# A shorter ending by column tiles of TensorE, ten unused matmuls in its waits, and two instruction programs aligned, in a decode attention kernel

## The chip, the cores and the metric

The kernel runs on one core of a Trainium2 chip. The metric is device time in microseconds, the median of several runs. The profile is one execution taken by the hardware profiler; its times count from the first instruction of that execution.

## The reference, cut to what matters

One decode step: two sequences of one token, a cached attention block with 32 heads of 8192 positions, and a small ReLU block beside it, both from the same normalised input.

```python
xn = _layernorm(x)                                    # x: [2, 1, 512]
# A: wq [512, 4096], K and V caches [2, 32, 8192, 128], wo [4096, 512]
q = (xn @ wq) per head                                # [2, 32, 1, 128]
p = softmax(q k^T * 128**-0.5);  o = p v
# B: w1 [512, 1792], w2 [1792, 512]
return x + o @ wo + relu(xn @ w1) @ w2
```

All inputs are bf16. K and V are 268 MB of the 280.5 MB that are read; wq, wo, w1 and w2 are the rest.

## The kernel before, in words

**The loop.** Sixteen turns work on four heads each. A turn brings 8 MB of K into the one buffer `ks` and 8 MB of V into the one buffer `vs`. TensorE transposes K (L278), VectorE and ScalarE copy the transposes out of PSUM (L446), TensorE makes the scores (L285), VectorE finds the maxima, ScalarE makes the exponentials with their sums in `RS`, and TensorE multiplies by V (L352). GpSimd hands out the queries of the next turn. All orders are written out by hand, with semaphores; there is no scheduler.

**The queue.** All large transfers are issued by SyncE on one queue, in program order: K, V, K, V and so on, and, as soon as the last K has been transposed, w1 (L191), w2 (L192) and wo (L195) into the space that K leaves in `ks`. wo comes in pieces along its 32 row groups `j`, cut at 0, 18, 26, 30 and 32, with one semaphore a piece, so that its product can begin before all of it is there. The matmuls of a piece wait for that piece (`piece[c]`).

**The ending**, after the last product with V, on TensorE in program order: the denominators (L373, four float32 matmuls against `onesh`); the input itself put into the accumulator `fin` (L379); the first product of the ReLU block (L390, 56 matmuls whose weights are w1 columns taken 14 elements apart, two columns of `xz` moving); the transposes of the attention output (L402); its move into the row layout of wo (L406); the second ReLU product (L417 from `hT`, 56 matmuls); the output projection (L417 from `OX`, 128 matmuls); a last transpose (L437). In L417 the weight matrix is TensorE's stationary operand, 128 columns at a time, and the two sequences are the two moving columns. VectorE works between these steps: the normalised output `OTn` (L511 to L529), the ReLU `hT` (L533), the copies `Ob` (L537), `OX` (L539), `yT` (L543) and `osb` (L545). SyncE then writes the output (L197).

**Unused matmuls.** `unused` (L308) multiplies the identity into a PSUM bank that nobody reads. The loop already has some in its waits.

Of the kernel before, what the change touches and what calls it, by code (L numbers as in the profile page):

```python
# [7 lines left out]
ALU = mybir.AluOpType  # L8
ACTF = mybir.ActivationFunctionType
AX = mybir.AxisListType  # L10

U = 4
# [4 lines left out]
TR = (21, 25)  # L17
BC = 32
FILL = 5
PZ = 4  # L20
ON_ACT = (0, 3, 5)


# [1 line left out]
def kernel(  # L25
# [35 lines left out]
    QG = H * Dh // 512  # L61
    QH = 512 // Dh
    Z = (QG - 1) * Bsz

    inv_sqrt = float(Dh) ** -0.5
    eps = 1e-5
# [3 lines left out]
    def sb(shape, dt, name):  # L70
        return ctx.enter_context(nc.sbuf_tensor(name, shape, dt))
# [4 lines left out]
    def sem(name):  # L76
        return tc.alloc_semaphore(name)
# [10 lines left out]
    kT = [sb([P, EG, P], bf16, f"kT{i}") for i in range(NG)]  # L88
    identb = sb([P, P], bf16, "identb")
    sel = sb([H, DQ, P], bf16, "sel")  # L90
    onesh = sb([P, U, P], f32, "onesh")
    onesb = sb([1, P], bf16, "onesb")
    eps_t = sb([P, 1], f32, "eps_t")
    xsb = sb([Bsz, D], bf16, "xsb")
# [3 lines left out]
    rinv = sb([Bsz, 1], f32, "rinv")  # L98
    xn = sb([Bsz, KT, P], bf16, "xn")

    xz = sb([P, KT, 2 * Z + Bsz], bf16, "xz")
    qs = sb([QG * Bsz, 512], bf16, "qs")
    qb = sb([P, N], bf16, "qb")
    q4 = sb([P, U], bf16, "q4")
# [2 lines left out]
    mcol = sb([P, 2], bf16, "mcol")  # L107
    mx = sb([1, 2, U], bf16, "mx")
    nm = sb([P, 2, U], f32, "nm")
    RS = sb([P, 2, NP], f32, "RS")  # L110
    NM = sb([P, 2, N], f32, "NM")
    OTf = sb([P, 2, N], f32, "OTf")
    lo = sb([P, N], f32, "lo")
# [6 lines left out]
    OG = sb([P, 2, N], f32, "OG")  # L120
    OTn = sb([P, Bsz, H], bf16, "OTn")
    Ob = sb([H, Bsz, Dh], bf16, "Ob")
    OX = sb([P, WJ, Bsz], bf16, "OX")
    hT = sb([P, FJ, Bsz], bf16, "hT")
    yT = sb([P, Bsz, KT], bf16, "yT")
    osb = sb([Bsz * KT, P], bf16, "osb")

# [23 lines left out]
    K_all = A_k_cache.rearrange("b h (m kk) d -> (b h m) (kk d)", kk=KB)  # L151
    V_all = A_v_cache.rearrange("b h (m kk) d -> (b h m) (kk d)", kk=KB)
    wo_v = A_wo.rearrange("(p j) n -> p j n", j=WJ)
    cuts = (0, 18, 26, 30, WJ)
    NC = len(cuts) - 1

    KSPLIT = (0, 2, NP - 1)
    VSPLIT = (1, 2)
    NL = 16 * NP
    piece = [(dX, 32), (dQ, 32)] + [(sem(f"dWo{c}"), 16) for c in range(2, NC)]  # L160
    qp = ot[0:QG * Bsz, :]
    tpq = ms[:, 0:N // 2].bitcast(bf16).rearrange("p (l c) -> p l c", l=QH)
    tpx = tp[0][:].rearrange("p g k -> p (g k)")[:, 0:KT * Bsz].rearrange(
        "p (kt b) -> p kt b", b=Bsz
    )
    hp = ms[:, 128:128 + FJ * Bsz].rearrange("p (j b) -> p j b", b=Bsz)
    ox = ms[:, 256:256 + Bsz * WJ]
    fin = Sc[:, 512:512 + KT * Bsz]

# [41 lines left out]

    @(lambda f: f(nc.gpsimd))
    def _(g):
        g.memset(identb[:], 0.0).then_inc(sG, 1)
        g.memset(sel[:], 0.0).then_inc(sG, 1)
        g.memset(onesh[:], 0.0).then_inc(sG, 1)
        g.wait_ge(sG, 1)
        g.affine_select(
            out=identb[:], in_=identb[:], compare_op=ALU.not_equal, fill=1.0,
            base=0, pattern=[[-1, P]], channel_multiplier=1,  # L220
        ).then_inc(sI, 1)
        g.wait_ge(sG, 2)
        g.affine_select(
            out=sel[:], in_=sel[:], compare_op=ALU.not_equal, fill=1.0,
            base=0, pattern=[[-1, DQ], [1, P]], channel_multiplier=-DQ,
        ).then_inc(sI, 1)
        g.wait_ge(sI, 2)
        for k in range(PZ - 1):
            g.memset(prm[:, k * KB // PZ:(k + 1) * KB // PZ, :], 0.0)
        g.memset(prm[:, KB - KB // PZ:KB, :], 0.0).then_inc(sG, 1)  # L230
        g.wait_ge(sG, 4)
        for u in range(U):
            g.memset(onesh[u * HP:(u + 1) * HP, u, :], 1.0).then_inc(sI, 1)
            g.wait_ge(sI, 3 + u)
        g.wait_ge(sV, 100)
        for t in range(NP):
            if t > 0:
                g.wait_ge(sS, 2 * t)
            g.tensor_copy(q4[:], qb[:, U * t:U * t + U]).then_inc(sQ1, 1)
            for d, split in ((dK, KSPLIT), (dV, VSPLIT)):  # L240
                if t not in split:
                    g.wait_ge(d[0], 16 * (t + 1)).then_inc(d[1], 16)
        g.wait_ge(dO, 16).then_inc(sG, 1)


    @(lambda f: f(nc.tensor))
    def _(pe):
# [119 lines left out]
                            warm(4)  # L367
            advance(pe, regs)

        pe.wait_ge(sI, 2 + U)  # L370
        dbp = Sc[:, 0:2 * N].rearrange("p (t u) -> p t u", u=U)
        for u in range(U):
            t = pe.matmul(  # L373
                dbp[:, :, u], lhsT=onesh[:, u, :], rhs=RS[:].rearrange("p i t -> p (i t)"),
                start=True, stop=True,
            )
        t.then_inc(sH, 1)
        for k in range(KT):
            pe.matmul(  # L379
                fin[:, k * Bsz:(k + 1) * Bsz],  # L380
                lhsT=xsb[:, k * P:(k + 1) * P],
                rhs=identb[0:Bsz, 0:Bsz],
                start=(k == 0),
                stop=False,
            )
        pe.wait_ge(dW1, 16)
        w1_v = w1_sb.rearrange("p kt (f j) -> p kt j f", j=FJ)
        for j in range(FJ):
            for kt in range(KT):
                i = pe.matmul(  # L390
                    hp[:, j, :],
                    lhsT=w1_v[:, kt, j, :],
                    rhs=xz[:, kt, Z:Z + Bsz],
                    start=(kt == 0),
                    stop=(kt == KT - 1),
                )
        i.then_inc(sF, 1)

        pe.wait_ge(sV, 108)
        tO = tp[0][0:H, 0:Bsz, :]  # L400
        for b in range(Bsz):
# [10 lines left out]
            )  # L412
        t.then_inc(sH, 1)

        def project(w, j, x, last=False):
            for k in range(KT):
                t = pe.matmul(  # L417
                    fin[:, k * Bsz:(k + 1) * Bsz],
                    lhsT=w[:, j, k * P:(k + 1) * P],
                    rhs=x[:, j, :],  # L420
                    start=False,
                    stop=(last and k == KT - 1),
                )
            return t

        pe.wait_ge(sF, 2)
        pe.wait_ge(dW2, 16)
        for j in range(FJ):
            project(w2_sb, j, hT)
        pe.wait_ge(sV, 110)  # L430
        for c in range(NC):
            pe.wait_ge(*piece[c])
            for j in range(cuts[c], cuts[c + 1]):
                t = project(wo_sb, j, OX, j == WJ - 1)
        t.then_inc(sH, 1)
        pe.wait_ge(sV, 111)
        pe.transpose(  # L437
            tp[1][0:Bsz * KT, 0, :], yT[:].rearrange("p b c -> p (b c)"), identb[:]
        ).then_inc(sH, 1)

    def kcopies(eng, act, h):
# [6 lines left out]

    @(lambda f: f(nc.vector))
    def _(v):  # L450
        v.memset(eps_t[:], eps).then_inc(sV, 1)
        v.memset(onesb[:], 1.0)
        v.memset(xz[:], 0.0).then_inc(sZ, 1)
        v.wait_ge(dX, 16)
        v.bn_stats(out=stats[:], in_=xsb[:]).then_inc(sV, 1)
        v.wait_ge(sV, 2)
# [50 lines left out]
        def both(ap):  # L507
# [21 lines left out]
        v.tensor_tensor(  # L529
            out=OTn[:].rearrange("p b h -> p (b h)"), in0=OG[:, 0, :], in1=OG[:, 1, :], op=ALU.add  # L530
        ).then_inc(sV, 1)
        v.wait_ge(sF, 1)
        v.tensor_scalar(  # L533
            out=hT[:], in0=hp, scalar1=0.0, scalar2=None, op0=ALU.max,
        ).then_inc(sF, 1)
        v.wait_ge(sH, 2)
        v.tensor_copy(Ob[:], tp[0][0:H, 0:Bsz, :]).then_inc(sV, 1)  # L537
        v.wait_ge(sH, 3)
        v.tensor_copy(  # L539
            OX[:], ox.rearrange("p (b j) -> p j b", b=Bsz)  # L540
        ).then_inc(sV, 1)
        v.wait_ge(sH, 4)
        v.tensor_copy(yT[:], fin.rearrange("p (c b) -> p b c", c=KT)).then_inc(sV, 1)  # L543
        v.wait_ge(sH, 5)
        v.tensor_copy(osb[:], tp[1][0:Bsz * KT, 0, :]).then_inc(sE, 1)  # L545


    @(lambda f: f(nc.scalar))
    def _(a):
        a.wait_ge(sV, 3)  # L550
        a.activation(
            out=rstd[:], in_=mv[:, 1:2], func=ACTF.Sqrt, bias=eps_t[:Bsz], scale=1.0
        ).then_inc(sA, 1)

        a.copy(nm[:, 0, 0:1], eps_t[:]).then_inc(sO, 1)
        regs = counters(a, mybir.EngineType.Activation)
        reg, g, h = regs[0], regs[1:3], regs[3:]
        with a.Fori(0, NP) as t:
            kcopies(a, True, h)
            for i in range(2):  # L560
                a.wait_ge(sB, g[i])
                a.copy(nm[:, i, :], bc[:, i, :]).then_inc(sN, 1)  # L562
                a.wait_ge(sN, g[i])
                for u in range(U):
                    own = slice(u * HP, (u + 1) * HP)
                    k = slice(i * KB // 2, (i + 1) * KB // 2)
                    x = a.activation(  # L567
                        out=prm[own, k, u],
                        in_=S[own, k, u],
                        func=ACTF.Exp,  # L570
                        bias=nm[own, i, u:u + 1],
                        scale=1.0,
                        accum_out=RS[own, i, bass.ds(t, 1)],
                    )
# [6 lines left out]
        a.activation(out=F[:], in_=df[:], func=ACTF.Exp, scale=1.0).then_inc(sA, 1)  # L581
# [1 line left out]
_INS = ['A_x', 'A_k_cache', 'A_v_cache', 'A_wq', 'A_wo', 'B_x', 'B_w1', 'B_w2']  # L583
_OUTS = [((2, 1, 512), 'bfloat16')]
# [25 lines left out]
```

## Time and profile before

| | us |
|---|---|
| median of 4 runs (658.56 to 658.89) | 658.58 |
| the profiled execution | 658.49 |
| its span, first to last instruction | 656.7 |
| last K transposed, w1 issued | 624.2 |
| last product with V ends on TensorE | 642.5 |
| last piece of wo landed | 653.04 |
| last matmul of the projection over | 653.48 |
| output write issued | 654.27 |

The profiled execution is 1.8 us longer than its span; that much lies around the first and last instruction. In the tables of the profile a row is a group of instructions: start, time, engine, line, operation, output and inputs, shapes, count, and in brackets the idle time of the engine before it. PE is TensorE's matmuls, PEld its weight loads, DVE is VectorE, ACT ScalarE, POOL GpSimd, SP SyncE. The time of one matmul in these rows runs from its start to the end of its passage; matmuls overlap, so what counts for a stream of them is the distance of their starts.

### The profile page before, as it was taken

The numbers are of one execution on the slowest core, as the hardware profiler recorded it, in microseconds if no ns is written. First come the engines' busy times: TensorE is split into PE (matmuls) and PEld (weight loads), VectorE is DVE, ScalarE is ACT, GpSimd is POOL, SyncE is SP. The second block draws the span as 40 slices with busy tenths as digits, with TensorE's granted clock in tenths as the row PEclk, the third lists the DMA queues.
The fourth block names the chain that finished last, engine by engine and source line by source line (L and its number), as shares of the span: only waits on it lengthen the run. The fifth ranks groups of instructions, "written<-read, shape, count | busy, mean of one in ns | idle before, by whom it ended". The sixth has DMA issues, their size and how long they took to land.

```text
span 656.7 us, 27972 instructions
## 1 busy us (share of the span) xinstructions
PE 611.4 (93%) x13071; PEld 540.0 (82%) x13071; DVE 261.8 (40%) x503; ACT 290.8 (44%) x532; POOL 7.2 (1%) x33
## 2 busy tenths in 40 slices
PE   2876999999999999999999999999999999999997
PEld 0575899968979798897969879796997979799987
DVE  1440353507235071633507154260715417072721
ACT  1332445526344363543527354353725435372730
POOL 2000000000000000000000000000000000000000
PEclk9998899999999999999999999999999999999997
DMA  9999999999999999999999999999999999999996
GB/s 381 450 437 413 418 431 431 461 415 431 431 435 427 443 427 439 427 435 443 423 435 435 435 443 423 427 431 447 427 439 423 435 443 423 431 431 424 459 393 288
DMA packets 6367, 280.66 MB, mean 427 GB/s; under 512 B 722, under 2 KB 724, under 8 KB 980
## 3 DMA queue, kind: packets, MB, share of 16 engines
q1 hardware_dynamic: 6352, 280.50, 99.0%
q8 instruction: 8, 0.13, 0.1%
q14 instruction: 3, 0.02, 0.0%
q10 hardware_dynamic: 4, 0.00, 0.0%
HBM read 280.50 MB, written 0.00 MB: 427 GB/s over the span
## 4 chain that ended last, share of the span: by engine, by line
DMA 54%; PE 43%; issue 2%; ACT 1%; SPq 0%; DVE 0%; ACTq 0%
DMA ks<-in_A_k_cache_dram 50%; PE tp L278 34%; DMA ks<-in_A_wo_dram 4%; PE ot L352 4%; PE Sc L285 4%; PE ms L308 1%; ACT L446 0%; DVE mcol L493 0%; ACT kT L446 0%; PE tp L308 0%; SPq L195 0%; PE ms L297 0%; PE ms L303 0%; SPq L192 0%; SPq L183 0%
## 5 line engine op out<-in xcount | busy, mean ns | idle before, releaser
L446 DVE COPY kT<-tp 128x1024 bf16<-128x1024 bf16 x320 | 209.1, 687 | 246.2 <-PE tp L278 240.5
L278 PEld LDWEIGHTS tp<-identb,ks 128*128 128x128 bf16 x4096 | 228.8, 98 | 22.4 <-DMA ks<-in_A_k_cache_dram 19.2
L278 PE MATMUL tp<-identb,ks 128*128 128x128 bf16 x4096 | 232.0, 219 | 15.5 <-DMA ks<-in_A_k_cache_dram 13.1
L446 ACT COPY kT<-tp 128x1024 bf16<-128x1024 bf16 x192 | 188.1, 1014 | 127.9 <-PE tp L278 127.8
L285 PE MATMUL Sc<-q,kT 128*128 128x64 bf16 (+8 forms) x4096 | 133.2, 191 | 4.5 <-issue 4.5
L352 PE MATMUL ot<-prm,vs 128*128 128x64 bf16 x4096 | 130.9, 193 | 3.8 <-issue 3.3
L285 PEld LDWEIGHTS Sc<-q,kT 128*128 128x128 bf16 x4096 | 128.6, 98 | 6.0 <-issue 4.8
L352 PEld LDWEIGHTS ot<-prm,vs 128*128 128x128 bf16 x4096 | 126.8, 97 | 5.8 <-issue 3.6
L308 PE MATMUL ms<-identb 128*128 128x512 bf16 x340 | 75.6, 379 | 0.0
L493 DVE TENSOR_REDUCE mcol<-Sc 32x1 bf16<-32x128 f32 x128 | 37.1, 290 | 93.9 <-PE Sc L285 92.6
L567 ACT ACTIVATE prm<-Sc,nm 32x128 bf16<-32x128 f32 x128 | 68.9, 539 | 5.4
L562 ACT COPY nm<-ms 128x4 f32<-128x4 f32 x32 | 5.2, 163 | 140.3 <-PE ms L303 140.3
L308 PEld LDWEIGHTS ms<-identb 128*128 128x128 bf16 x340 | 32.4, 98 | 37.1 <-issue 0.2
L578 ACT COPY OTf<-ot 128x8 f32 x16 | 2.6, 165 | 72.7 <-PE ot L352 72.7
L567 ACT ACTIVATION_READ_ACCUMULATOR prm<-Sc,nm x128 | 32.1, 251 | 0.0
L446 ACT ACT_TABLE_LOAD x16 | 20.5, 1283 | 3.7 <-issue 3.6
L308 PE MATMUL tp<-identb 128*128 128x512 bf16 x80 | 20.8, 391 | 0.0
L257 PE MATMUL ot<-vs,xz 128*16 128x512 bf16 x32 | 9.8, 482 | 8.6 <-DMA vs<-in_A_wq_dram 8.6
L257 PEld LDWEIGHTS ot<-vs,xz 128*16 128x16 bf16 x32 | 3.4, 107 | 14.6 <-issue 12.6
L500 DVE TENSOR_REDUCE mx<-ms 1x4 bf16<-1x128 bf16 x32 | 8.9, 279 | 14.3 <-PE ms L297 14.3
L297 PEld LDWEIGHTS ms<-identb,mcol 128*1 128x1 bf16 x32 | 2.5, 79 | 12.8 <-ACT prm L567 11.2
L308 PEld LDWEIGHTS tp<-identb 128*128 128x128 bf16 x80 | 6.7, 98 | 6.2 <-issue 0.8
(64 smaller groups left out, 57.3 us busy)
## 6 DMA issues: line engine op xcount, KB each, us to landing
ks<-in_A_k_cache_dram SPq DMA_DIRECT2D x6, 4096.0 KB, 22.3
vs<-in_A_v_cache_dram SPq DMA_DIRECT2D x4, 4096.0 KB, 21.6
vs<-in_A_wq_dram SPq DMA_DIRECT2D x1, 4096.0 KB, 12.3
ks<-in_B_w_dram SPq DMA_DIRECT2D x2, 1792.0 KB, 16.4
ks<-in_A_wo_dram SPq DMA_DIRECT2D x1, 2304.0 KB
ks<-in_A_wo_dram SPq DMA_DIRECT2D x1, 1024.0 KB, 25.6
ks<-in_A_wo_dram SPq DMA_DIRECT2D x1, 512.0 KB, 26.4
ks<-in_A_wo_dram SPq DMA_DIRECT2D x1, 256.0 KB, 26.6
```

Of the source, the lines that this page charges most:

```text
L257: i = pe.matmul(qp, lhsT=xz[:, kt, Z - g * Bsz:Z - g * Bsz + QG * Bsz], rhs=vs[:, (kt * QG + g) * 512:(kt * QG + g + 1) * 512], start=(g = ...
L278: t = pe.transpose(tp[e % 4][:, i, :], ks[:, kk * Dh:(kk + 1) * Dh], identb[:])
L285: t = pe.matmul(Sc[:, U * kk:U * (kk + n)], lhsT=kT[e][:, i, :], rhs=rep(q4[:], n), start=True, stop=True,)
L297: pe.transpose(trp[:, i * P:(i + 1) * P], mcol[:, i:i + 1], identb[:]).then_inc(sT, 1)
L308: pe.matmul(out, lhsT=identb[:], rhs=identb[:].rearrange("p (o k) -> p o k", o=1).to_broadcast([P, 4, P]), start=True, stop=True,)
L352: t = pe.matmul(oh[:, i, :], lhsT=vs[:, kk * Dh:(kk + 1) * Dh], rhs=rep(prm[:, kk, :], REP), start=(first == 0), stop=(first == KB // 2 - 1),)
L446: fn(kT[e][:], tp[e % 4][:]).then_inc(kR[e % HG], 1)
L493: m = v.tensor_reduce(out=mcol[own, i:i + 1], in_=S[own, i * KB // 2:(i + 1) * KB // 2, u], axis=AX.X, op=ALU.max,)
L500: v.tensor_reduce(out=mx[:, i, :], in_=trp[:, i * P:(i + 1) * P].rearrange("o (u m) -> o u m", u=U), axis=AX.X, op=ALU.max, negate=True,). ...
L562: a.copy(nm[:, i, :], bc[:, i, :]).then_inc(sN, 1)
L567: x = a.activation(out=prm[own, k, u], in_=S[own, k, u], func=ACTF.Exp, bias=nm[own, i, u:u + 1], scale=1.0, accum_out=RS[own, i, bass.ds( ...
L578: a.copy(OTf[:, :, bass.ds(t * U, U)], oh[:, :, 0:U]).then_inc(sO, 1)
```

## The change

The ending is rewritten; the loop stays as it is. Three products change sides: the few columns of the activations become the stationary operand, filled up to 32 columns with zeros, and the weight matrix moves past, 448 or 512 columns in one matmul. Each such matmul uses a quarter of TensorE's columns and writes 32 partitions of PSUM, and consecutive matmuls go round the four quarters. This holds for w1 (16 matmuls), w2 (14) and the first 22 of 32 row groups of wo. The four partial sums in `y` are copied by VectorE to `ys` and added by four float32 matmuls against the selection `sel2`. The last ten row groups of wo are done in the old way. wo is cut at 0, 14, 22, 26, 30 and 32, five pieces. Seven unused matmuls follow the first piece and three the second. w1's product is copied by ScalarE (`hb`), transposed by 14 small matmuls, and the ReLU is done in four instructions, one for each quarter. The denominators need one float32 matmul, because `RS` now has a column for each head. GpSimd sets `RS`, `ones`, `hT` and `OX` to constants. The programs of VectorE and GpSimd begin with an instruction to the loader to place them at a multiple of 128 instructions, with a branch over what lies between.

```diff
+FETCH = 128
+PAUSE = (7, 3)
-    cuts = (0, 18, 26, 30, WJ)
+    cuts = (0, 14, 22, 26, 30, WJ)
+    WIDE = 2
@@ GpSimd
+        g.addr_align(FETCH, max_nops=0)
...
+        g.memset(RS[:], 0.0).then_inc(sG, 1)
+        g.memset(ones[:], 1.0).then_inc(sG, 1)
+        g.memset(hT[:], 0.0).then_inc(sG, 1)
...
+        g.wait_ge(sS, 2 * NP)
+        g.memset(OX, 0.0).then_inc(sI, 1)
@@ TensorE
-        for u in range(U):
-            t = pe.matmul(dbp[:, :, u], lhsT=onesh[:, u, :], rhs=RS[:]...)
+        pe.matmul(Sc[:, 0:2 * N], lhsT=ones[:], rhs=RS[:]...).then_inc(sH, 1)
         pe.wait_ge(dW1, 16)
-        for j in range(FJ):
-            for kt in range(KT):
-                i = pe.matmul(hp[:, j, :], lhsT=w1_v[:, kt, j, :], rhs=xz[:, kt, Z:Z + Bsz], ...)
+        for kt in range(KT):
+            for c in range(TC):
+                i = pe.matmul(tile(hp, c)[:, 0:FJ * CT], lhsT=xz[:, kt, Z:Z + CT],
+                    rhs=w1_sb[:, kt, c * FJ * CT:(c + 1) * FJ * CT], ...)
+        pe.matmul(tile(y, 0), lhsT=identb[0:Bsz, 0:CT], rhs=xsb[:], start=True, stop=False)
+        pe.wait_ge(sF, 2)
+        for j in range(FJ):
+            t = pe.matmul(hq[...], lhsT=hb[:, j, :], rhs=rows, start=True, stop=True)
...
-        for j in range(FJ):
-            project(w2_sb, j, hT)
+        for j in range(FJ):
+            pe.matmul(tile(y, j % TC), lhsT=hT[:, j, :], rhs=w2_sb[:, j, :], ...)
         pe.wait_ge(sV, 110)
-        for c in range(NC):
-            pe.wait_ge(*piece[c])
-            for j in range(cuts[c], cuts[c + 1]):
-                t = project(wo_sb, j, OX, j == WJ - 1)
+        for i in range(WIDE):
+            pe.wait_ge(*piece[i])
+            for j in range(cuts[i], cuts[i + 1]):
+                t = pe.matmul(tile(y, j % TC), lhsT=OX[:, j, :], rhs=wo_sb[:, j, :], ...)
+            if i == WIDE - 1:
+                t.then_inc(sH, 1)
+            for k in range(PAUSE[i]):
+                unused(ms[:])
+        for i in range(WIDE, NC):
+            if i == WIDE:
+                pe.wait_ge(sF, 5)
+                for k in range(KT):
+                    pe.matmul(fin[:, k * Bsz:(k + 1) * Bsz],
+                        lhsT=ys[:, k * P:(k + 1) * P], rhs=sel2[:], ...)
+            pe.wait_ge(*piece[i])
+            for j in range(cuts[i], cuts[i + 1]):
+                for k in range(KT):
+                    t = pe.matmul(fin[...], lhsT=wo_sb[:, j, k * P:(k + 1) * P],
+                        rhs=OX[:, j, 0:Bsz], ...)
@@ VectorE
+        v.addr_align(FETCH, max_nops=0)
+        v.wait_ge(sI, 1)
+        v.tensor_reduce(out=sel2[:], in_=identb[:]..., op=ALU.add)
...
-        v.tensor_scalar(out=hT[:], in0=hp, scalar1=0.0, op0=ALU.max).then_inc(sF, 1)
+        for c in range(TC):
+            m = v.tensor_scalar(out=hT[c * CT:(c + 1) * CT, :, 0:Bsz],
+                in0=hq...[:, :, c, :], scalar1=0.0, op0=ALU.max)
+        m.then_inc(sF, 1)
...
+        v.tensor_copy(ys, y).then_inc(sF, 1)
@@ ScalarE, after the loop
+        a.wait_ge(sF, 1)
+        a.copy(hb, hp[:, 0:FJ * CT].rearrange("p (f j) -> p j f", j=FJ)).then_inc(sF, 1)
```

More of the change, by code (lines that the diff above doesn't have):

```diff
@@ L19 @@
 FILL = 5
-PZ = 4
+CT = 32
+FETCH = 128
+PAUSE = (7, 3)
 ON_ACT = (0, 3, 5)
@@ L63 @@
     Z = (QG - 1) * Bsz
+    TC = P // CT
+    assert D == 512 and FJ * CT <= 512 and FJ * TC * Bsz <= 512
     inv_sqrt = float(Dh) ** -0.5
@@ L90 @@
     sel = sb([H, DQ, P], bf16, "sel")
-    onesh = sb([P, U, P], f32, "onesh")
+    ones = sb([P, P], f32, "ones")
     onesb = sb([1, P], bf16, "onesb")
@@ L99 @@
     xn = sb([Bsz, KT, P], bf16, "xn")
-    xz = sb([P, KT, 2 * Z + Bsz], bf16, "xz")
+    xz = sb([P, KT, max(2 * Z + Bsz, Z + CT)], bf16, "xz")
     qs = sb([QG * Bsz, 512], bf16, "qs")
@@ L109 @@
     nm = sb([P, 2, U], f32, "nm")
-    RS = sb([P, 2, NP], f32, "RS")
+    RS = sb([P, 2, NP, U], f32, "RS")
     NM = sb([P, 2, N], f32, "NM")
@@ L122 @@
     Ob = sb([H, Bsz, Dh], bf16, "Ob")
-    OX = sb([P, WJ, Bsz], bf16, "OX")
-    hT = sb([P, FJ, Bsz], bf16, "hT")
+    hT = sb([P, FJ, CT], bf16, "hT")
+    sel2 = sb([P, Bsz], f32, "sel2")
     yT = sb([P, Bsz, KT], bf16, "yT")
@@ L159 @@
     NL = 16 * NP
-    piece = [(dX, 32), (dQ, 32)] + [(sem(f"dWo{c}"), 16) for c in range(2, NC)]
+    piece = [(dX, 32), (dQ, 32), (dK[0], NL + 16), (dK[1], NL + 16)] + [
+        (sem(f"dWo{c}"), 16) for c in range(4, NC)
+    ]
     qp = ot[0:QG * Bsz, :]
@@ L165 @@
     )
-    hp = ms[:, 128:128 + FJ * Bsz].rearrange("p (j b) -> p j b", b=Bsz)
+    hp = tp[2][:].rearrange("p g k -> p (g k)").bitcast(f32)
+    y = tp[1][:].rearrange("p g k -> p (g k)").bitcast(f32)
+    hb = kT[0][:].rearrange("p g k -> p (g k)")[:, 0:FJ * CT].rearrange(
+        "p (j f) -> p j f", j=FJ
+    )
+    hq = tp[3][:].rearrange("p g k -> p (g k)").bitcast(f32)[0:CT, 0:FJ * TC * Bsz]
+    OX = kT[2][:].rearrange("p g k -> p (g k)").rearrange("p (j c) -> p j c", c=CT)
+    ys = kT[1][:].rearrange("p g k -> p (g k)").bitcast(f32)
     ox = ms[:, 256:256 + Bsz * WJ]
@@ L213, in _ @@
     def _(g):
+        g.addr_align(FETCH, max_nops=0)
         g.memset(identb[:], 0.0).then_inc(sG, 1)
         g.memset(sel[:], 0.0).then_inc(sG, 1)
-        g.memset(onesh[:], 0.0).then_inc(sG, 1)
         g.wait_ge(sG, 1)
@@ L227, in _ @@
         g.wait_ge(sI, 2)
[L228 to L231, printed above, removed]
-        for u in range(U):
-            g.memset(onesh[u * HP:(u + 1) * HP, u, :], 1.0).then_inc(sI, 1)
-            g.wait_ge(sI, 3 + u)
+        g.memset(prm[:], 0.0).then_inc(sG, 1)
+        g.memset(RS[:], 0.0).then_inc(sG, 1)
+        g.memset(ones[:], 1.0).then_inc(sG, 1)
+        g.memset(hT[:], 0.0).then_inc(sG, 1)
+        g.wait_ge(sG, 6)
         g.wait_ge(sV, 100)
@@ L368, in _, with tile @@
             advance(pe, regs)
[L370 to L385, printed above, removed]
+        pe.matmul(
+            Sc[:, 0:2 * N], lhsT=ones[:], rhs=RS[:].rearrange("p i t u -> p (i t u)"),
+            start=True, stop=True,
+        ).then_inc(sH, 1)
+        def tile(ap, c):
+            return ap[c * CT:(c + 1) * CT, :]
         pe.wait_ge(dW1, 16)
-        w1_v = w1_sb.rearrange("p kt (f j) -> p kt j f", j=FJ)
-        for j in range(FJ):
-            for kt in range(KT):
+        for kt in range(KT):
+            for c in range(TC):
                 i = pe.matmul(
-                    hp[:, j, :],
-                    lhsT=w1_v[:, kt, j, :],
-                    rhs=xz[:, kt, Z:Z + Bsz],
+                    tile(hp, c)[:, 0:FJ * CT],
+                    lhsT=xz[:, kt, Z:Z + CT],
+                    rhs=w1_sb[:, kt, c * FJ * CT:(c + 1) * FJ * CT],
                     start=(kt == 0),
@@ L397, in _ @@
         i.then_inc(sF, 1)
+        pe.matmul(
+            tile(y, 0), lhsT=identb[0:Bsz, 0:CT], rhs=xsb[:], start=True, stop=False
+        )
+        pe.wait_ge(sF, 2)
+        rows = identb[:].rearrange("p (c r) -> p c r", c=TC)[:, :, 0:Bsz]
+        for j in range(FJ):
+            t = pe.matmul(
+                hq[:, j * TC * Bsz:(j + 1) * TC * Bsz].rearrange("p (c b) -> p c b", c=TC),
+                lhsT=hb[:, j, :], rhs=rows, start=True, stop=True,
+            )
+        t.then_inc(sF, 1)
         pe.wait_ge(sV, 108)
@@ L413, in _ @@
         t.then_inc(sH, 1)
[L415 to L426, printed above, removed]
+        pe.wait_ge(sF, 4)
         pe.wait_ge(dW2, 16)
         for j in range(FJ):
-            project(w2_sb, j, hT)
-        pe.wait_ge(sV, 110)
-        for c in range(NC):
-            pe.wait_ge(*piece[c])
-            for j in range(cuts[c], cuts[c + 1]):
-                t = project(wo_sb, j, OX, j == WJ - 1)
+            c = j % TC
+            pe.matmul(
+                tile(y, c), lhsT=hT[:, j, :], rhs=w2_sb[:, j, :],
+                start=(0 < j < TC), stop=False,
+            )
+        pe.wait_ge(sV, 110)
+        for i in range(WIDE):
+            pe.wait_ge(*piece[i])
+            for j in range(cuts[i], cuts[i + 1]):
+                t = pe.matmul(
+                    tile(y, j % TC), lhsT=OX[:, j, :], rhs=wo_sb[:, j, :],
+                    start=False, stop=(j >= cuts[WIDE] - TC),
+                )
+            if i == WIDE - 1:
[6 more added lines that the diff above has]
+                for k in range(KT):
+                    pe.matmul(
+                        fin[:, k * Bsz:(k + 1) * Bsz],
+                        lhsT=ys[:, k * P:(k + 1) * P],
+                        rhs=sel2[:],
+                        start=(k == 0),
+                        stop=False,
+                    )
+            pe.wait_ge(*piece[i])
+            for j in range(cuts[i], cuts[i + 1]):
+                for k in range(KT):
+                    t = pe.matmul(
+                        fin[:, k * Bsz:(k + 1) * Bsz],
+                        lhsT=wo_sb[:, j, k * P:(k + 1) * P],
+                        rhs=OX[:, j, 0:Bsz],
+                        start=False,
+                        stop=(j == WJ - 1 and k == KT - 1),
+                    )
         t.then_inc(sH, 1)
@@ L437, in _ @@
         pe.transpose(
-            tp[1][0:Bsz * KT, 0, :], yT[:].rearrange("p b c -> p (b c)"), identb[:]
+            tp[0][0:Bsz * KT, Bsz, :], yT[:].rearrange("p b c -> p (b c)"), identb[:]
         ).then_inc(sH, 1)
@@ L453, in _ @@
         v.memset(xz[:], 0.0).then_inc(sZ, 1)
+        v.wait_ge(sI, 1)
+        v.tensor_reduce(
+            out=sel2[:],
+            in_=identb[:].rearrange("p (c r) -> p r c", c=TC)[:, 0:Bsz, :],
+            axis=AX.X, op=ALU.add,
+        )
         v.wait_ge(dX, 16)
@@ L531, in _ @@
         ).then_inc(sV, 1)
[L532 to L535, printed above, removed]
+        v.wait_ge(sF, 3)
+        for c in range(TC):
+            m = v.tensor_scalar(
+                out=hT[c * CT:(c + 1) * CT, :, 0:Bsz],
+                in0=hq.rearrange("p (j c b) -> p j c b", j=FJ, c=TC)[:, :, c, :],
+                scalar1=0.0, scalar2=None, op0=ALU.max,
+            )
+        m.then_inc(sF, 1)
         v.wait_ge(sH, 2)
@@ L538, in _ @@
         v.wait_ge(sH, 3)
+        v.wait_ge(sI, 3)
         v.tensor_copy(
-            OX[:], ox.rearrange("p (b j) -> p j b", b=Bsz)
+            OX[:, :, 0:Bsz], ox.rearrange("p (b j) -> p j b", b=Bsz)
         ).then_inc(sV, 1)
         v.wait_ge(sH, 4)
+        v.tensor_copy(ys, y).then_inc(sF, 1)
+        v.wait_ge(sH, 5)
         v.tensor_copy(yT[:], fin.rearrange("p (c b) -> p b c", c=KT)).then_inc(sV, 1)
-        v.wait_ge(sH, 5)
-        v.tensor_copy(osb[:], tp[1][0:Bsz * KT, 0, :]).then_inc(sE, 1)
+        v.wait_ge(sH, 6)
+        v.tensor_copy(osb[:], tp[0][0:Bsz * KT, Bsz, :]).then_inc(sE, 1)
     @(lambda f: f(nc.scalar))
@@ L572, in _ @@
                         scale=1.0,
-                        accum_out=RS[own, i, bass.ds(t, 1)],
+                        accum_out=RS[own, i, bass.ds(t, 1), u],
                     )
@@ L581, in _ @@
         a.activation(out=F[:], in_=df[:], func=ACTF.Exp, scale=1.0).then_inc(sA, 1)
+        a.wait_ge(sF, 1)
+        a.copy(
+            hb, hp[:, 0:FJ * CT].rearrange("p (f j) -> p j f", j=FJ)
+        ).then_inc(sF, 1)
 _INS = ['A_x', 'A_k_cache', 'A_v_cache', 'A_wq', 'A_wo', 'B_x', 'B_w1', 'B_w2']
```

## The prediction

> **What bounds the kernel now.** I read the chain that ended last, then the ending in order of time, then windows of 3.41 us for the clock, then the queues.
>
> ```profile
> 626.49 26.56 DMA ks<-in_A_wo_dram
> 653.04 0.05 issue
> 653.09 0.38 PE Sc L417 x8
> 653.50 0.18 DVE yT L543
> 653.72 0.28 PE tp L437
> 654.03 0.21 DVE osb L545
> ```
>
> The last piece of wo lands at 653.04 and the rest hangs on it: 8 matmuls, a copy, a transpose, a copy, the output write. The page's DMA row shows nines in every slice but the last: the end is 280.5 MB through a queue that does not pause. But TensorE is nearly as late:
>
> ```profile
> 642.45 1.07 PE L373 MATMUL Sc<-RS,onesh 128*128 128x32 f32 x8
> 642.90 0.31 ACT L581 ACTIVATE F<-df 128x128 f32<-128x128 f32 x1
> 643.64 3.52 PE L390 MATMUL ms<-xz,ks 128*128 128x2 bf16 x56
> 645.54 0.22 DVE L529 TENSOR_TENSOR OTn<-OG 128x64 bf16<-128x64 f32 x1
> 647.09 0.40 PE L402 MATMUL tp<-identb,OTn 128*32 128x128 bf16 x2
> 647.20 0.19 DVE L533 TENSOR_SCALAR hT<-ms 128x28 bf16<-128x28 f32 x1 [1.43 <-PE ms L390]
> 647.52 0.28 DVE L537 COPY Ob<-tp 32x256 bf16<-32x256 bf16 x1
> 647.86 0.39 PE L406 MATMUL ms<-Ob,sel 32*128 32x64 bf16 x4 [0.38 <-DVE Ob L537]
> 648.18 1.65 PE L417 MATMUL Sc<-hT,ks 128*128 128x2 bf16 x56
> ```
>
> From 642.45 TensorE idles 0.4 us in all before 653. The projection's starts are 0.0267 us apart from 649.69 to 652.88; only the last piece shows a wait, 0.19 us. So all TensorE time removed ahead of it is worth nothing by itself; it becomes waiting for wo. The columns of the next view are length, busy time of PE, PEld, DVE, ACT and POOL, granted clock, DMA share, GB/s.
>
> ```profile
> 643.66:647.07 3.41, 3.41 (x58) 3.41 (x56) 1.78 (x6) 0.00 (x0) 0.00 (x0) 1.00 0.98 414
> 647.07:650.48 3.41, 3.03 (x94) 2.67 (x94) 0.69 (x3) 0.00 (x0) 0.00 (x0) 0.50 0.94 382
> ```
>
> A window of w1 matmuls, two columns wide each, is followed by half clock to the end. Before, that costs nearly nothing: starts 0.0267 us apart at half clock against 0.025 in L379 at full.
>
> **Part 1: when wo is there.** The queues for 650 to 653.2:
>
> ```profile
> q1 hardware_dynamic: 256, 0.65, 51.6%
> q8 instruction: 1, 0.02, 2.1%
> ```
>
> Between the data lie instruction fetches. The trace has two of 16 KB for q8, at 646.67 (1.07 us) and 651.21 (1.08), and one of 8 KB at 648.53 (0.32). In the packets an engine's data stop while it fetches. Of the last piece's sixteen landing marks the last three are at 652.77, 652.79 and 653.04: the last belongs to an engine with a late fetch. TensorE started 125 weight-matmul pairs between the two, so q8 is its program, a fetch each 256 or so instructions. After the loop there were 259 pairs; afterwards there are 134 (two passes for each float32 one). The first fetch came after 63 pairs, so it stays, and the second falls behind the end. The landing comes 0.25 earlier, at 652.79. The fifth piece adds a SyncE issue of 0.43 us at 626.9, with V still in flight until 634.35, and 4 KB packets: 8 of 18 KB took 5.50 us, 8 of 14 KB and 8 of 4 KB 4.29 and 1.26, so 0.05 more. **Landing 652.84, gain 0.20.**
>
> **Part 2: TensorE's way there.** Starting at 642.45:
> - Denominators: two passes for eight. A pass takes 0.11 (L373); between 0.2 and all of 1.07 I take 0.3, as two passes are nearest. VectorE then waits for F, ready at 643.21, and all of its chain is 0.30 earlier: OTn ends 645.46. At the other end (1.07) it is unmoved.
> - w1: 56 x 0.060 = 3.4 us become 16 of 448 columns. The trace has no matmul on a quarter of the columns beside another; the nearest rows are L308 and L257 (128x512), 0.216 apart at full clock, so 0.19 each. One after the other 3.0; four at once 0.76. I take four at once, 643.6 (why: last rival).
> - hb: ScalarE's 128x1024 copy takes 1.01 and its 128x8 copy 0.17, so 0.54 for 448. Fourteen small matmuls at 0.027 (L417) to 0.05 (L406) are 0.4 to 0.7. Done by 645.1; OTn at 645.46 hides it with 0.36 to spare, and beyond that each us is a us.
> - VectorE: four hT at 0.19 and 0.03 of gap are 0.88, for 0.32; Ob queues behind them and starts at 646.40. From Ob's start to the second ReLU product were 0.66 us: it starts at 647.06, before 648.18.
> - w2 and wo's first piece: 28 x 0.216/4 = 1.5, to 648.57; one after the other 6.0.
> - Seven unused at 0.216: to 650.08. The second piece lands at 649.6 (633.89, when the last engine ends V, + 24 x 0.536 + 8 x 0.309 + 0.42 to the mark), so they overrun it by 0.45.
> - Second piece 0.43, then 0.19 of passage, then ys: the nearest copy is L475, 0.68, of 512 float32 columns; three unused (0.65) lie beside it. 651.4.
> - Adding y: eight passes at 0.112, 0.9: 652.3. 32 old-style matmuls 0.85: 653.15. The last eight begin then, not at 652.89 (landing and 0.05), and their last start is 653.34, against 653.30 before.
>
> So the cut leaves TensorE, not wo, in front, by 0.25, and the sum is +0.04 on the path. Each late row (hT, unused, ys) is rounded up, and at the lower ends TensorE waits for wo: -0.20. I take half-way, -0.08. The last transpose at full clock (0.22 in L297, 0.27 in L437) gives 0.05 if the clock holds.
>
> **Part 3: constants and alignment.** GpSimd's OX is four times a 0.25 us memset, after the last V lands at 634.35, needed at 647: eleven us of cover. Its other memsets and VectorE's sel2 wait for the identity lie before xz, ready at 4.97, while L257 starts on wq at 13.37: 8.4 us of cover; without it each would cost its 0.1 to 1 us. The branch over the padding is between nothing and a fetch, 0.33, under the same cover. The 8 KB fetches at 599.84 and 648.53 follow GpSimd's L239 and VectorE's L539; neither is followed by a stall, so losing them gains nothing there. A fetch moved onto or off the engine that ends last is 0.33 later or earlier; I take 0. In the loop the queue never pauses, so a shifted VectorE loop is hidden too: w1 was issued 10 us before V had landed.
>
> Sum: 658.49 - 0.08 - 0.05 + 0 = 658.36; the median lay 0.09 above this execution, so **658.4**, called no change.
>
> **A rule weighed.** The Trainium skill, "TensorE: Matmul & The Clock Gate", Part 1, has activity windows of 3.41 us that run free of the kernel, the clock halving after an idle one. The windows above agree (647.07 is such an edge); that the edge falls elsewhere in another run, no run here shows. By the page the first rival below would be a matter of luck in each run; by the row alone it is a matter of this run's edge.
>
> **Rivals.**
> 1. *Slower: half clock where it now matters.* From the end of w1 (643.8) to 647.06 TensorE now does almost nothing: 14 matmuls of 8 columns, six small ones. In the loop, windows with 1.71 of 3.4 us busy (49.7 to 53.2) and 0.89 (63.4 to 66.8) were each followed by half clock. If a window ends between about 646 and 648, the wide matmuls run at 0.43 (L257 before 19.0): 28 x 0.108 = 3.0 to 650.08 instead of 648.57. The clock is back at 650.5, after one unused matmul; six more, 651.8; second piece 652.25; +0.19 + 0.68 + 0.9 + 0.85 + 0.21 = 655.05 against 653.30. **+1.75, 660.2.** For: the two loop windows, and the row after 643.66. Against: an edge elsewhere leaves part of w1 or w2 in each window. It decides once the first piece ends after 649.3 or so. Chance 0.20.
> 2. *Slower: quarters one after the other.* w1 ends 645.85, hb, its matmuls and hT at 648.3, w2 from 649.0, 28 x 0.216 to 655.0, unused 656.5, second piece 658.25, then 0.19 + 0.68 + 0.9 + 1.06: 661.1. **+7.8, 666.3.** For: L308 and L257 show no overlap, but all on the same columns. Against: a matmul 128 columns wide and 2 deep starts each 0.027 while passing takes 0.165, so the array holds several at once. Chance 0.04. The page named above (Part 3) measured 2.38 for three column tiles; by it, as an estimate, 28 would take 1.9 us, 0.4 more than my sum.
> 3. *Faster by over 0.2%.* All fetches gone, the landing is 652.79 at best, and behind it 0.05 is removed; 1.3 us more would need the first engines' mark, 651.14, for all. Chance 0.03.
> 4. *It doesn't do what it says:* TensorE is shorter but never in front. That is the lower end of the forecast, 658.3, -0.25; inside it.
>
> **How the numbers follow.** The forecast has 0.73: within 0.2% (1.3 us, about what a measurement of this kernel can tell from no change). Its own range is 657.9 (-0.25, one fetch off the last engine -0.33) to 659.3 (+0.04, 0.4 for imperfect quarters, 0.33 a fetch). The half-clock rival spreads from 659.3 to 661, centre 660.2; two thirds of it lie above 659.9, which with the one-after-the-other case is 0.17 slower. The range reaches to its centre: 657.9 to 660.3, leaving out 0.08 of it, 0.04 and 0.03.
>
> **What would show it.** Right: one q8 fetch after 640, none of 8 KB by VectorE; wo landed at 652.8; w1 matmuls about 0.05 apart; the second ReLU product near 647.1; last eight matmuls around 653.1. Wrong: wide matmuls 0.1 apart or a clock of 0.5 after 647 (rival 1); 0.2 apart (rival 2); the last landing before 652.5; a VectorE stall at the ReLU.

## The result, and the profile after

The changed kernel takes 659.96 us, median of 41 runs, against 658.76 for the kernel before (66 runs beside it): ratio 1.0018 [1.0012, 1.0024]. It is slower by 1.2 us, and the forecast of no change, 658.4, was wrong; the time is that of the first rival (660.2). The 41 runs don't spread evenly: 8 lie between 658.26 and 658.93, one at 659.17, 25 between 659.64 and 660.71, 7 between 661.81 and 662.83. These groups are what has to be explained. The execution profiled here took 660.0, span 658.2 (before: 658.49 and 656.7), so it stands for the largest group. Long runs are not the change's alone: 4 of the 66 of the kernel before lie between 660.7 and 662.3.

The chain that ended last (start, us, what):

```profile
645.93 0.29 DVE Ob L585
646.22 0.05 issue
646.27 0.28 PE ms L422 x4
646.55 1.59 PE tp L435 x14
648.15 1.71 PE tp L443 x14
649.85 1.79 PE ms L322 x7
651.65 0.55 PE tp L443 x8
652.19 0.75 PE ms L322 x3
652.95 0.04 issue
652.99 1.05 PE Sc L455 x8
654.04 1.01 PE Sc L465 x40
655.06 0.02 issue
655.08 0.18 DVE yT L594
```

Before, the chain ended with a transfer, wo, at 653.04. Now no transfer is in it: from 646.27 to 655.06 it is TensorE matmul after matmul. wo's second piece landed at 649.57 and had to wait until 651.6; the last piece landed at 652.71, and its eight matmuls start from 654.71 to 654.88. The page's clock row, in slices of 16.5 us, shows 8 tenths in its last slice where before it showed 7. It is too coarse to show what follows. The ending in order of time:

```profile
642.75 0.94 PE L395 MATMUL tp<-ks,xz 128*32 128x448 bf16 x16
645.16 0.74 DVE L578 TENSOR_SCALAR hT<-tp 32x28 bf16<-32x28 f32 x4
646.49 1.66 PE L435 MATMUL tp<-ks,hT 128*32 128x512 bf16 x14
647.52 2.33 PE L443 MATMUL tp<-ks,kT 128*32 128x512 bf16 x14
649.79 1.86 PE L322 MATMUL ms<-identb 128*128 128x512 bf16 x7
651.58 0.61 PE L443 MATMUL tp<-ks,kT 128*32 128x512 bf16 x8
```

The 28 wide matmuls of w2 and wo's first piece take 3.3 us, from 646.49 to 649.79, where the sum had 1.5. Then the windows 642.4 to 646.5, 646.5 to 649.8 and 649.8 to 653.2; columns as in the prediction's view (length, busy PE, PEld, DVE, ACT, POOL, granted clock, DMA share, GB/s):

```profile
642.40:646.50 4.10, 2.62 (x43) 1.35 (x44) 2.78 (x11) 1.01 (x3) 0.00 (x0) 1.00 1.01 422
646.50:649.80 3.30, 3.30 (x31) 1.13 (x30) 0.23 (x1) 0.00 (x0) 0.00 (x0) 0.54 0.98 395
649.80:653.20 3.40, 3.35 (x22) 1.15 (x20) 0.69 (x1) 0.00 (x0) 0.00 (x0) 0.94 0.54 210
```

The thinly used stretch ran at full clock and the wide matmuls behind it at 0.54. In the trace the clock falls to 0.5 at 646.76, for 3.41 us, and is 1.0 again from 650.17. The wide matmuls start in rounds, in up to four quarters at once: the first two rounds, ahead of that edge, 0.225 apart, the later ones 0.427.

### The profile page after: what moved, and what is told of

Its sections match the earlier page's. It is cut to its first block, busy times and chain, and to the rows that moved or that the text cites. A ratio compares the mean times of both kernels' runs of the same rounds, so it can differ in the third digit from the quotient of the medians.

```text
span 658.2 us, 27728 instructions
## 1 busy us (share of the span) xinstructions
PE 611.2 (93%) x12946; PEld 535.6 (81%) x12946; DVE 263.0 (40%) x508; ACT 291.3 (44%) x533; POOL 7.6 (1%) x29
## 4 chain that ended last, share of the span: by engine, by line
DMA 58%; PE 39%; DVE 1%; ACT 0%; issue 0%; SPq 0%; ACTq 0%; DVEq 0%
DMA ks<-in_A_k_cache_dram 55%; PE tp L292 32%; DMA vs<-in_A_v_cache_dram 4%; PE ot L366 4%; PE Sc L299 2%; PE ms L322 0%; DVE mcol L537 0%; PE tp L443 0%; PE tp L435 0%; ACT L483 0%; PE Sc L455 0%; ACT kT L483 0%; PE Sc L465 0%; PE ms L311 0%; DVE hT L578 0%
## 5 line engine op out<-in xcount | busy, mean ns | idle before, releaser
L322 PE MATMUL ms<-identb 128*128 128x512 bf16 x350 | 78.2, 379 | 0.0
```

The source lines that it names most:

```text
L322: pe.matmul(out, lhsT=identb[:], rhs=identb[:].rearrange("p (o k) -> p o k", o=1).to_broadcast([P, 4, P]), start=True, stop=True,)
```

## The experiments

Two theories stood against each other. *Half clock*: one window, entered behind the thin stretch, makes w2 and wo dear, and nothing else in the change costs anything. *The chain itself*: the new way (quarters, copy of the sums, adding by float32 matmuls, unused matmuls, alignment) is too long at any clock. The first four runs share the kernel before at 658.64, the next two at 658.82, the last one 658.76.

**Cover of the thin stretch.** Seven more unused matmuls are put in the waits ahead of w2; nothing is taken out.

```diff
+COVER = (2, 2, 3)
...
+        for k in range(COVER[0]):     # before the wait for hb
+            unused(ms[:])
...
+        for k in range(COVER[1]):     # before the wait for OTn
+            unused(ms[:])
...
+        for k in range(COVER[2]):     # before the wait for Ob
+            unused(ms[:])
```

> The changed kernel with seven more unused matmuls of 512 columns in TensorE's three waits between the w1 product and the second ReLU product: two before the wait for hb, two before the wait for OTn, three before the wait for Ob. In the profile after, those waits are 0.7, 0.6 and 0.8 us, so 7 x 0.216 = 1.5 us fit in. Theory (the ending runs at half clock because the 3.4 us window before it holds almost no matmul columns): the clock stays at 1.0 through 647 to 650.5, the 28 wide matmuls take 1.5 us and not 3.3, the last eight matmuls start when the last piece lands (652.7), and the median falls from 660.0 to about 658.3, with no runs near 660. Rival 1 (the price lies in the aligned programs or in instruction fetches): stays at 660.0. Rival 2 (unused matmuls are the delay themselves): at least 660, more by whatever of the seven sticks out of the waits.

Measured: 658.9 (11 runs, ten of them 658.28 to 659.33, one 661.17), ratio 1.0004 [0.9992, 1.0015]. The crowd of runs near 660 is gone; the expected 658.3 was not reached. The windows and the wide matmuls of the covered kernel (its L442 is w2, L450 wo, L323 the unused ones):

```profile
642.40:646.50 4.10, 4.10 (x46) 1.67 (x46) 2.78 (x11) 1.01 (x3) 0.00 (x0) 1.00 0.98 412
646.50:649.80 3.30, 3.30 (x39) 1.38 (x35) 0.22 (x1) 0.00 (x0) 0.00 (x0) 1.00 1.00 403
```

```profile
646.53 1.04 PE L442 MATMUL tp<-ks,hT 128*32 128x512 bf16 x14
647.20 1.24 PE L450 MATMUL tp<-ks,kT 128*32 128x512 bf16 x14
648.37 1.68 PE L323 MATMUL ms<-identb 128*128 128x512 bf16 x7
649.98 0.62 PE L450 MATMUL tp<-ks,kT 128*32 128x512 bf16 x8
```

TensorE is busy for all 4.10 us of the first stretch, and the clock stays full until 654.80. w2 starts at the same place (646.53 against 646.49), so the added work delayed nothing; the 28 wide matmuls take 1.84 instead of 3.30, and the second piece starts at 649.98 instead of 651.58. These 1.6 us are the loss: the profiled last starts before and after stand 1.58 apart (653.30, 654.88). What is left is no gain over before. This execution's window edges, counted back from 654.80, lie at 644.56 and 647.97, where no profiled run of the change had one, so by itself it leaves open whether cover or edge kept the clock up; the kernel with five unused matmuls, below, settles that.

**No pauses.** Without the ten unused matmuls behind w2, and without cover.

```diff
-PAUSE = (7, 3)
+PAUSE = (0, 0)
```

> The changed kernel without its ten unused matmuls. Theory (half clock): the half-clock window after the w1 product remains, w2 and the first piece still take 3.3 us to 649.8, but the 1.8 us of unused matmuls at half and full clock are gone, and the second piece begins at 649.8, when it has landed: about 1.7 us earlier than after, so 658.4 to 658.7, nearly the same in both clock cases. Rival 2 (the unused matmuls are the delay, whatever the clock): the same fall, but then the profile's clock in 647 to 650.5 would be 1.0. Rival 1 (alignment or fetches): stays at 660.0. If the ten were what kept the clock up for the float32 sum and the last 40 matmuls, those would now be at half clock: their starts 0.22 and 0.027 us apart, +0.9 us.

Measured: 659.45 (658.22 to 660.72), ratio 1.0008 [0.9996, 1.0020]; not to be told from before, nor well from after. In order of time:

```profile
646.61 1.89 PE L435 MATMUL tp<-ks,hT 128*32 128x512 bf16 x14
647.87 3.19 PE L443 MATMUL tp<-ks,kT 128*32 128x512 bf16 x22
651.85 1.87 PE L455 MATMUL Sc<-sel,kT 128*128 128x2 f32 x8 [0.79 <-DVE kT L592]
```

The second piece no longer queues behind unused work, and its last wide matmul is over at 651.1 instead of 652.2. But the clock is 0.5 from 645.72 to the end, and the float32 matmuls that add the four parts take 1.87 instead of 1.05, their passes 0.213 apart instead of 0.112. The expected 658.4 to 658.7 was missed by 0.8; the last clause of the expectation, the adding at half clock, is what came. The second rival would have needed full clock in 646.5 to 649.8; it was 0.50. So the pauses cost when the clock has fallen, and give part of it back in the adding. They are not the cause.

**Alignment, both ways.** The change without it, and the kernel before with it alone.

```diff
-        g.addr_align(FETCH, max_nops=0)
...
-        v.addr_align(FETCH, max_nops=0)
```

> The changed kernel without the two alignment instructions. Theory (half clock): the same as the changed kernel, 659.9 to 660.1 in the median, with a few runs near 658.4. Rival 1 (alignment costs the time): falls to 658.5. A third case: without alignment VectorE or GpSimd crosses a fetch boundary in the ending and stalls for a fetch, 0.3 to 1.5 us later than the changed kernel.

> The kernel before with only the two alignment instructions. Theory: the same as before within 0.2 us; VectorE starts 0.5 us later, covered by the 8 us until wq lands. Rival 1 (alignment costs the time): +1.2 us.

Measured: without it 660.3 (12 runs), ratio 1.0017 [1.0005, 1.0029], as after; alone 658.71, ratio 1.0001 [0.9990, 1.0012], as before. No effect of the alignment shows either way. The aligned kernel before no longer had the 8 KB instruction fetches at 599.84 and 648.53, and its time did not change: the step that put those fetches at no price held.

**Narrow w2 and wo.** w1 stays in quarters, with its short stretch of work; w2 and wo go the old way, two columns moving, without `ys`, adding or pauses, wo cut as before.

```diff
-    cuts = (0, 14, 22, 26, 30, WJ)
+    cuts = (0, 18, 26, 30, WJ)
...
-            pe.matmul(
-                tile(y, c), lhsT=hT[:, j, :], rhs=w2_sb[:, j, :],
...
+            project(w2_sb, j, hT)
```

> The changed kernel with w1 by quarters and one float32 matmul for the denominators, but w2 and all of wo in the old way (two moving columns, four matmuls a row group), no partial sums, no unused matmuls, wo cut as before. Theory (half clock is dear for wide matmuls alone): w2 begins at 646.5; 56 starts 0.027 us apart to 648.0, then wo as it lands, whatever the clock; the last eight start when the last piece lands, 652.7 to 652.8. 658.2 to 658.4, no runs near 660 although the profile shows a clock of 0.5. Rival (the price is in what the change does before w2: the quarters of w1, ScalarE's copy, four ReLU instructions): about 660.

Measured: 658.65 (658.18 to 659.31), ratio 0.9995 [0.9983, 1.0007]; no run near 660. Its matmuls in order of time:

```profile
646.41 1.57 PE L432 MATMUL Sc<-hT,ks 128*128 128x2 bf16 x56
649.00 2.06 PE L432 MATMUL Sc<-kT,ks 128*128 128x2 bf16 x72 [1.02 <-DMA ks<-in_A_wo_dram]
651.40 1.01 PE L432 MATMUL Sc<-kT,ks 128*128 128x2 bf16 x32 [0.34 <-DMA ks<-in_A_wo_dram]
652.64 1.01 PE L432 MATMUL Sc<-kT,ks 128*128 128x2 bf16 x24 [0.23 <-DMA ks<-in_A_wo_dram]
```

The clock was 0.5 from 647.51 to the end here too. It did no harm: in the old way a row group takes four starts, 0.107 us, at half clock, and TensorE now waits for wo three times. So the thin stretch and the half clock do not cost by themselves; they cost what runs wide behind them. A round of four wide matmuls takes 0.216 at full clock, 0.054 a row group, and 0.427 at half, 0.107 a row group: at half clock the wide way loses its whole advantage. At full clock, 36 row groups that take 3.85 us in the old way take ten rounds (why not nine, below), 2.16 us: 1.7 saved. Passage, copy of the sums (0.69 + 0.19) and adding (0.9) take 1.8 back. This kernel is faster than the change and not to be told from the one before: wo's last landing, 653.23, ends it. The expected 658.2 to 658.4 had this landing at 652.7 to 652.8.

**Cover with fewer pauses, and with none.** If TensorE was still in front of wo in the covered kernel, taking two or all seven unused matmuls away should show.

```diff
-PAUSE = (7, 3)
+PAUSE = (5, 3)      # and (0, 0) in the other one
+COVER = (2, 2, 3)
```

> The kernel with seven more unused matmuls in the early waits, and five, not seven, after the first piece of wo. In the profile of the kernel with seven and seven, those after the first piece end at 649.9 while the second piece lands at 649.5, and TensorE is late from there to the end. Theory: the second piece starts 0.4 us earlier, the last eight matmuls start at 652.7, and the time falls by 0.3 to 0.4 us to 658.3 to 658.5, no runs near 660. Rival (unused matmuls cost nothing where they stand, and what is left over the best runs is the queue): unchanged at 658.9.

> The changed kernel with the seven unused matmuls in the early waits and without its own ten. Theory: the clock of the stretch that holds the wide matmuls is decided by the stretch before it, so the seven are the ones that matter: w2 and 14 row groups take 1.5 us to 648.1, the second piece starts as it lands, and the median is 658.3 to 658.8, no worse than with the ten. Rival (the ten keep the clock up as well): in some runs the float32 sum and the last 40 matmuls fall to half clock, 0.22 us a pass and not 0.11, which costs 0.9 us, and the median is above 659.

Measured: 658.83, ratio 1.0002 [0.9994, 1.0011], and 658.71, ratio 1.0003 [0.9994, 1.0011]. The hoped-for 0.3 to 0.4 us did not come. Of the 34 runs of the three covered kernels, three lie above 660 (660.37, 660.71, 661.17), against 32 of 41 of the change above 659.6. With five, the second piece waits for wo (0.18 us, landing 650.19) and the last piece landed at 653.31. Its window edge, counted back by 3.41 us from a fall at 655.86 to 649.03 and 645.62, lies between two edges at which the change fell to half clock (645.43 and 645.70, next experiment). Here the clock stays full, in the stretch of the wide matmuls too:

```profile
646.50:649.80 3.30, 3.10 (x37) 1.15 (x35) 0.23 (x1) 0.00 (x0) 0.00 (x0) 1.00 0.98 397
```

So it is the cover, and not a lucky edge, that kept it up. With none, TensorE waits 1.14 us for wo, and the rows in order of time show the price of a later window instead:

```profile
649.55 0.61 PE L450 MATMUL tp<-ks,kT 128*32 128x512 bf16 x8 [1.14 <-DMA ks<-in_A_wo_dram]
650.97 1.85 PE L462 MATMUL Sc<-sel,kT 128*128 128x2 f32 x8 [0.80 <-DVE kT L599]
```

The clock falls at 651.03, just when the adding starts, and it takes 1.85. In the profiled execution this puts the last start 0.43 later than in the first covered kernel (653.89 against 653.46 for the end of the chain's narrow matmuls); the medians do not show it. For the wide matmuls it is the seven unused ones ahead of w2 that matter, not the ten behind it.

**The change again, four times.** The same kernel, unchanged, to see whether the group of a run goes with the place of the edge.

> The changed kernel once more, for another edge of the clock's windows. Theory: if the first window edge after 644 lies where half clock covers the wide matmuls, w2 and the first piece take over 3 us and the run is near 660.0; if two windows are at half, the unused matmuls are slow too, near 661.7; if none of that stretch is at half, w2 starts at 646.5, ends its 28 at 648.0, and the run is near 658.4. Rival (the time has another cause): time and clock of that stretch don't go together.

> The same kernel a second time, with the same expectation: 660.0 with one half-clock window over the 28 wide matmuls, about 661.7 with two, 658.4 with none.

> The changed kernel for a third edge of the clock's windows: 660.0 with one half-clock window over the 28 wide matmuls, about 661 with two, 658.4 with none.

> The same for a fourth edge: 660.0 with one half-clock window over the 28 wide matmuls, about 661 with two, 658.4 with none.

Measured: 660.06, 661.16, 659.68 and 660.08; for two windows 661.7 had been expected at first. The clock fell at 646.37, 645.43, 645.70 and 646.31; three times for one window of 3.41 us, in the second for two (6.83). That second execution, in order of time and in its last window:

```profile
649.98 2.79 PE L322 MATMUL ms<-identb 128*128 128x512 bf16 x7
652.70 0.61 PE L443 MATMUL tp<-ks,kT 128*32 128x512 bf16 x8
```

```profile
649.80:653.20 3.40, 3.40 (x17) 1.01 (x15) 0.00 (x0) 0.00 (x0) 0.00 (x0) 0.64 0.53 208
```

The unused matmuls, 1.86 in the first profile, take 2.79 here, and the second piece starts 1.1 later: they are meant to keep TensorE busy while it waits and are themselves the longest thing in the way once a second window is slow. No execution from the group near 658.5 was profiled; the covered kernels, which bring that case about, stand in for it. Of the group above 661.8 none was profiled either. Two half windows give 661.16; the kernel without alignment was profiled at 662.57 with two half windows and V landed 0.8 us later than usual, 635.02. That the whole upper group is this, is not shown.

## Why the prediction was wrong, step by step

**The step that failed is the term for w2 and wo's first piece.** The prediction put it at full clock, 28 x 0.216/4 = 1.5 us. It measured 3.30, because the clock was 0.5 from 646.76 on (and because the 28 are eight rounds, not seven, see Part 2). The prediction had this case as rival 1, priced it, and gave it a chance of 0.20. The rival's place, mechanism and price were right:

| | rival 1 predicted | measured |
|---|---|---|
| wide matmuls, distance in the quarter | 0.43 | 0.427 |
| w2 and first piece, us | 3.0 | 3.3 |
| last start | 655.05 | 654.88 |
| time | 660.2 | 660.0 (median 659.96) |

That the last start came so close is in part luck: w2 began 0.57 earlier than worked out, and its rounds took 0.3 longer. The chance of 0.20 does not follow from the prediction's own condition, that a window ends between about 646 and 648. The one edge it had read, 647.07, lies inside. With windows of 3.41 us whose edges can fall anywhere, it is 2 of 3.41, 0.59. Either way the rival was the likeliest case and should have been the forecast. Instead the text let "an edge elsewhere leaves part of w1 or w2 in each window" stand for most of the chance. The condition was also too narrow: edges at 645.43, 645.70, 646.31, 646.37 and 646.76 all made the change slow, and 32 of 41 runs lie above 659.6. The range, 657.9 to 660.3, holds the 659.96 only because it was drawn out to the rival's centre. And 0.2% is not the least that can be told from no change: the interval of the ratio is 0.12% wide.

The prediction left open whether the edge falls elsewhere in another run. It does. Over the profiles of this case edges of the ending stand, among others, at 645.24, 645.43, 645.70, 646.31, 646.76, 647.08, 647.51 and 647.97 (counted back by 3.41 us where the clock changed at a later edge), spread over 2.7 of the 3.41 us. The Trainium skill, "TensorE: Matmul & The Clock Gate", Part 1, whose windows run free of the kernel, is borne out by these runs; taken at its word it would have given the 0.59.

**The window's measure.** The argument from busy time in the loop was loose. The prediction's own row, 643.66 to 647.07 before, was busy 3.41 of 3.41 us and still followed by half clock, so "the windows above agree" holds for the window's length and edge and not for an idle window, if idle is read from the busy time. The matmuls of that row move two columns each. Count only the time in which columns move in at least one quarter, at 0.42 ns a column in either state of the clock (0.216 us for 512). Then that window holds a share of 0.01. For the endings profiled:

| window of 3.41 us | share with columns moving | next window |
|---|---|---|
| before; before with alignment; narrow w2 and wo | 0.01; 0.20; 0.09 | half |
| change, five profiles | 0.27 to 0.39 | half |
| without pauses; without alignment | 0.37; 0.37 | half |
| second window: without pauses, without alignment, the change at 661.16 | 0.43 each | half |
| second window: the change, the other four | 0.45 to 0.54 | full |
| covered, without pauses, 647.61 to 651.03 | 0.32 | half |
| three covered kernels, their earlier windows from 640.8 on | 0.57 to 0.85 | full |

Counted so over all windows of the thirteen traces, none above 0.43 was followed by half clock and none below 0.39 by full clock. From 0.39 to 0.43 both occur: 0.39 from 46.33 to 49.74 in the kernel before was followed by full clock, 0.43 in the table by half. So the share orders the windows, and no exact limit is shown. No experiment set the share on purpose apart from the cover.

**Part 1, landing.** The second q8 fetch did fall away: the trace after has one, at 646.27. The last landing was 652.71 (predicted 652.84). But in the other profiles of the change and the covered kernels it lies between 652.61 and 653.46, with the same single fetch, and one or two of the sixteen last marks stand up to 0.8 behind the others. The 0.20 is real in the count and not to be relied on in the time. "None of 8 KB by VectorE" is not settled: one of 8 KB stands at 646.33, 0.38 us, whose engine the trace does not name.

**Part 2, TensorE.** The chain up to w2 was overestimated: it started at 646.49, not 647.06. The ReLU in four took 0.74, not 0.88, and `OTn` ended at 645.24, not 645.46. The denominators took 0.41 to the next start, not 0.3. w1 at four quarters at once (rounds 0.189 apart, 0.94 with the last passage), `hb` (0.53), `ys` (0.69) and the adding (0.91 to the next start, predicted 0.9) came as worked out. A term was missing: the 28 wide matmuls are eight rounds, not 28/4 = seven. w2 has 14 row groups, and wo's first group goes to the first quarter again (`j % TC`), so two quarters get eight matmuls and two get six. In the covered kernel the last pair starts at 648.05 and not, as the last of seven rounds would, at 647.84. The first full-width unused matmul follows at 648.37, 0.31 after that pair, 0.1 more than a round. At full clock the sum still came out: w2 begins 0.53 earlier than predicted there, the second piece 0.10 earlier, the adding at 651.39 (predicted 651.4), the last eight matmuls at 653.11 (predicted 653.15). These are errors that cancel. The last landing was 652.63 in that execution, so TensorE, not wo, is in front by 0.4, where the sum had 0.25. The point "last eight matmuls around 653.1" holds there and not in the change (654.71).

**Part 3** held: constants, alignment and the branch cost nothing that a run showed, though VectorE's first memset started at 1.56 instead of 1.02; `xz` was ready at 5.1, far ahead of its use.

**Rival 2** is refuted: quarters start 3 to 4 ns apart. The page weighed there (Part 3, 2.38 for three column tiles) is bettered by the trace, whose four tiles run side by side within a stream, in rounds 0.216 apart. **Rival 3** did not come. Neither did **rival 4** (TensorE never in front): TensorE ends the chain in the change and in the covered kernel. With narrow w2 and wo, wo ends it.

## What to carry to other kernels

Before narrow matmuls are turned into wide ones, look at how much column-moving work stands in the 3.4 us ahead of them, not at how busy TensorE looks there: here narrow ones, at their distance of 0.025 to 0.027, hardly changed with the clock, wide and float32 ones took nearly twice as long. If a wait is left open there, fill it with unused wide matmuls ahead of the work, and do not put more of them behind it than its wait can hold at half clock. Here this brought the time back to that of the kernel before, not below it. Count rounds by the fullest quarter, not by the mean of the four. When a rival comes with a condition, work out the share of runs that meet it before giving it a chance.

## What the runs showed of the hardware that was not expected

- A window in which TensorE is busy all the time with two-column matmuls (3.41 of 3.41 us) was followed by half clock; columns moved in 0.01 of it.
- The edge of the window wanders from run to run over at least 2.7 of 3.41 us, and the change has groups of times, near 658.5, 660 and 662; the profiles tie the one near 660 to the place of the edge.
- A float32 pass with 128 columns of weights starts each 0.112 us at full clock and each 0.213 at half; a two-column bf16 pair each 0.025 and 0.0267.
- The last landing of the same load varies by 0.85 us (652.61 to 653.46) over seven executions, each with one 16 KB and one 8 KB instruction fetch after 640.
